# An inverse step joined to another unit's head, its banks emptied by ScalarE, and split and weight sums spread

## The chip, the cores and the metric

The kernel runs on one core of a Trainium2 chip. The metric is the time of one execution on the device in microseconds; three runs of the kernel before are given. A profile of one execution goes with them.

## What is computed

```python
def _attn_ref(x, filt_r, filt_i):          # x: (8, 3008, 256)
    X = np.fft.rfft(x, axis=1)
    Y = X * (filt_r + 1j * filt_i)[None, :, :]
    return np.fft.irfft(Y, n=x.shape[1], axis=1).astype(np.float32)

def _moe_ref(x, w_in, w_out):              # x: (24064, 256), w_in: (256, 2048), w_out: (2048, 256)
    h = x @ w_in
    g = h - np.tanh(h)
    return (g @ w_out).astype(np.float32)
```

The output of the first function, with batch and sequence flattened, is the input of the second. All is float32; the weights come as 64-bit floats and are converted on the chip.

## The kernel before, in words

**The transform.** The sequence of 3008 is 64 x 47. The forward transform has a first step (`first`, or `split_first` from batch 3 on, in small tiles), which goes to DRAM (`ct1`), and a middle step (`middle`): products over the 47 residues, the filter, products back, and out to DRAM again (`ct2`). `middle` does this four times per batch; each time has a "there" (products by `packed` with the first of `WAYS`, line 407), eight steps of filter arithmetic on VectorE, and a "back" (`packed` with the second of `WAYS`). The inverse's last step is `last`: it reads `e2` (loaded from `ct2` by `load_e2`) and makes `ut`, the activations of the dense part, with 32 products in tiles of 64 x 64 (64 instructions, line 587).

**The dense part.** Batches are cut into six chunks; a pair of batch and chunk is a group, 48 in all. A group is worked in four units `U = 4 i + u`, each with a quarter of the hidden columns. In unit `U` TensorE does `up(U)` and `down(U - 2)`, while `shrink(U - 1)` computes h - tanh(h) on ScalarE and VectorE. Both products use seven block products in place of eight, so combinations of blocks are formed beforehand: of weights by `sums`, of activations by `combine` on POOL or VectorE. `up` has banks `x`, `y` and `z`; `down` accumulates in `o0` to `o3` from a group's unit 2 to the next group's unit 1; one more bank is `t`.

**The order.** It is written out by hand. `up` calls four callbacks between its products: `d` and `e` advance `down`, `s` advances `shrink`, and `t(k)`, k = 0 to 4, advances everything else at a fixed place in the unit: up to four stores, then one of: the next group's `last` at (unit 3, k = 2), a step of `first` for batch 2, a step of `split_first` for batch p + 2 at the places in `SPLIT_AT` (chunk, unit, k), or a step of `middle` for batch p + 1 ("there" at (2, 0), "back" at (1, 3), filter arithmetic at `FILTERED`). The conversion of the weights and their sums go on in `t` and `e` by `converting`, from a generator `late`.

**Banks around the change.** `up` begins with products 1 and 2 into `x` and `y`, whose reader is the copy `s1` and the addition of line 651; `t(0)` comes after them. The last value of `x` is read by the copy of line 676, after the fourth call of `t`. `last` uses banks `t` and `y`; ScalarE copies the odd one (line 591) and VectorE adds and subtracts, reading the even one from the bank (lines 594 and 595). "there" uses `t`, `o3`, `o1`, `o2`; ScalarE copies the last two, and VectorE reads the first two from the banks (lines 491 and 492). In unit 1, `down` for the group before ends; its last bank, `o3`, is read by VectorE at line 839. A split's products have line 346, its copies lines 351 and 352, its sums lines 354 and 355.

Of the kernel before, what the change touches and what calls it, by code (L numbers as in the profile page):

```python
# [9 lines left out]
F32 = mybir.dt.float32  # L10
# [7 lines left out]
BATCH, SEQ, DM = 8, 3008, 256  # L18
# [6 lines left out]
CH = 4  # L25
XH = 4
NC = NH // CH
# [90 lines left out]
def kernel(  # L118
# [104 lines left out]

        return jobs

    def sums(u):

        w = (wu if u < 4 else wd)[:, :, 256 * (u % 4):256 * (u % 4) + 256]
        V.tensor_add(w[:, 4], w[:, 6], w[:, 3])
        yield  # L230
        for to, one_in, less in ((5, 4, 0), (2, 1, 5), (6, 0, 6)):
            V.tensor_sub(w[:, to], w[:, one_in], w[:, less])
            yield

    def begun(tiles, job, queue=nc.sync):
        j = converted(tiles, *job, queue)
# [3 lines left out]
    pending = [1]  # L240
# [71 lines left out]
    def split_first(b, z):  # L312

        quarters = [slice(32 * k, 32 * k + 32) for k in range(4)]
        for c, tags in enumerate((("t", "o1", "y", "o0"), ("t", "o3", "o1", "o2"),
                                  ("t", "o1", "y", "o0"))):
            f = tr.tile([128, XH, 128], F32, tag="f", bufs=2, name="f")[:, 0:2]
            f = f.rearrange("p a (b n) -> p (a b) n", n=32)
            nc.sync.dma_start(f, split_d[:, 256 * c:256 * c + 256])
            x0, x1 = (tr.tile([128, XH, DM], F32, tag="x", bufs=2, name="x_sb") for _ in range(2))  # L320
            for h, t in enumerate((x0, x1)):
                at = b * SEQ + 32 * h * NR
                for g in range(2):
                    r = 2 * FH * c + FH * g
                    low, high = quarters[g], quarters[2 + g]
                    nc.sync.dma_start(t[low], dram(x.tensor, (at + r) * DM,
                                                   [[NR * DM, 32], [1, FH * DM]]))
                    lo = int(r == 0)
                    if lo:
                        nc.sync.dma_start(t[high, 0], dram(x.tensor, at * DM,  # L330
                                                           [[NR * DM, 32], [1, DM]]))
                    nc.sync.dma_start(t[high, lo:FH], dram(x.tensor, (at + NR - r - lo) * DM,
                                                           [[NR * DM, 32], [-DM, FH - lo], [1, DM]]))
            yield
            both = tr.tile([128, 2, 2, DM], F32, tag="a1", bufs=1, name="a1")
            even = both.rearrange("p v n c -> p (v n) c")
            V.tensor_add(even, x0, x1)
            yield
            V.tensor_sub(x1, x0, x1)
            yield  # L340
            banks = z(tags)
            for n in range(2):
                for k, (bank, part) in enumerate(zip(banks, quarters)):
                    for j, to in enumerate(quarters):
                        m, odd = 2 * (j // 2) + n, j % 2
                        nc.tensor.matmul(bank[to, n], f[part, 2 * m + odd],  # L346
                                         (x1 if odd else even)[part, m], start=True, stop=True)
            made = both, x0.rearrange("p (v n) c -> p v n c", v=2)
            other = x1[:, 0:2]
            for g, a1 in enumerate(made):  # L350
                ACT.copy(a1[:, 1], banks[2 + g])
            ACT.copy(other, banks[1])
            for g, a1 in enumerate(made):
                V.tensor_add(a1[:, 0], other if g else banks[0], a1[:, 1])
                V.tensor_sub(a1[:, 1], other if g else banks[0], a1[:, 1])
                outs[:0] = [(dram(ct1[b], ((1 - j % 2) * NH + 2 * FH * c + FH * g +
                                           2 * (j // 2)) * DM,
                                  [[2 * NH * DM, 32], [64 * NH * DM, 2], [1, 2 * DM]]),
                             a1[part].rearrange("p v n c -> p v (n c)"))
                            for j, part in enumerate(quarters)]  # L360
                yield

    SPLIT_AT = {(0, 0, 2), (0, 1, 0), (0, 1, 3), (1, 1, 1), (1, 1, 4), (2, 0, 2),
                (3, 0, 2), (4, 2, 0), (4, 2, 2), (4, 3, 0), (5, 0, 2), (5, 1, 0), (5, 1, 3),
                (5, 2, 2)}

    def parts(t, b, g, first_block=0, n=4, step=1):

# [24 lines left out]
    def packed(banks, o, weight, data):  # L393

        ahead, whole, late = [], [], []
        for q, bank in enumerate(banks):
            part = slice(PAD * q, PAD * q + NH)
            for col in range(4):
                to, at = bank[PAD * col:PAD * col + PAD], data(q, col)[part]
                plain, special = (wide[part, weight(q, col, last)] for last in (0, 1))  # L400
                if o == 3 and 3 == (col if weight is WAYS[0] else q):
                    ahead.append((to[:, 0], plain, at[:, 0:DM]))
                    late.append((to[:, 1], special, at[:, DM:2 * DM]))
                else:
                    whole.append((to.rearrange("p n c -> p (n c)"), plain, at))
        for to, weights_of, at in ahead + whole + late:
            nc.tensor.matmul(to, weights_of, at, start=True, stop=True)  # L407
# [165 lines left out]

    e2s, uts = {}, {}

    def last(i, z):

        b, c = groups[i]
        n = sum(widths(c))
# [3 lines left out]
        for h in range(2):  # L583
            for j, r in enumerate(order(c)):
                for bank, half in zip(banks, rows):
                    for m, part in enumerate(rows):
                        nc.tensor.matmul(bank[part, h, j],  # L587
                                         e2[half, r - CH * c, h * 128 + 64 * m:h * 128 + 64 * m + 64],
                                         gt[half, r - CH * c], start=True, stop=True)
        odd = tr.tile([128, 2, CH, 64], F32, tag="e1", bufs=2, name="odd")  # L590
        ACT.copy(odd, banks[1])
        u4 = ut.rearrange("p h (j n) -> p h j n", n=128)
        m = sum(w == 128 for w in widths(c))
        V.tensor_add(u4[:, :, :, 0:64], banks[0], odd)
        V.tensor_sub(u4[:, :, 0:m, 127:63:-1], banks[0][:, :, 0:m], odd[:, :, 0:m])
        w = n // 2
        if i == 0:
            uts[i] = (ut, None, w)
# [13 lines left out]

    hs, gs = {}, {}

    def up(U, d, e, s, t):

        i, u = divmod(U, 4)
        b, tu, w = uts[i]
        rhs = [b[0][0], b[1][0], b[1][1], tu[:, 3, 0:w], tu[:, 0, 0:w], tu[:, 1, 0:w],
               tu[:, 2, 0:w]]  # L620
# [24 lines left out]
        mm(X, 1, True)  # L645
        mm(Y, 2, True)
        s1 = copied("s1")
        t(0)
        d()
        shrinks(0)  # L650
        V.tensor_add(h[:, 0, :, 0:w], Y, s1)
# [76 lines left out]
    def shrink(U):  # L728
# [42 lines left out]
        if U + 2 == 4 * len(groups):  # L771
            yield

        combine(blocks, [t[:, k, :, 0:w] for k in range(4)],
                V if pending or U + 2 >= 4 * len(groups) else G)
        gs[U] = (blocks, t, w)
        yield

# [232 lines left out]
    with tc.tile_pool(name="tr", bufs=2) as tr, tc.manual_schedule():  # L1011
# [278 lines left out]
        with tc.tile_pool(name="dn", bufs=2) as dn, \  # L1290
# [5 lines left out]
            def zd2(name, shape):  # L1296
                return [ps.tile(shape, F32, tag=tag, bufs=1, name=name) for tag in "ty"]

            def zd4(tags):
                return [ps.tile([128, 2, DM], F32, tag=tag, bufs=1, name="pm") for tag in tags]  # L1300

# [55 lines left out]
            kinds.update({at: "filter" for at in FILTERED})  # L1357

            firsts, mids = {2: fs}, {}
            for U in range(total + 2):  # L1360
                i, u = divmod(U, 4)
                if U == 6:
                    assert not pending
                    late = (None for u in (3, 5, 6, 7) for _ in sums(u))
                if U == 3:
                    G.dma_start(mats[:, 0:10 * PAD], wide_d[0:KM])
                if U < total:
                    p, c = groups[i]
                    if c == 0 and u == 0 and 0 < p < BATCH - 1:
                        plan += STAGES  # L1370
                    if u == 0 and i + 1 < len(groups) and c + 1 < NC:
                        e2s[i + 1] = load_e2(*groups[i + 1])
                    if u == 2 and i + 1 < len(groups) and c + 1 == NC:
                        assert not plan
                        e2s[i + 1] = load_e2(*groups[i + 1])
                    if u == 3 and c + 1 == NC and p + 3 < BATCH:
                        firsts[p + 3] = split_first(p + 3, zd4)
                        next(firsts[p + 3])
                    if u == 3 and c + 1 == NC and p + 2 < BATCH:
                        mids[p + 2] = middle(p + 2, zd4)  # L1380
                        next(mids[p + 2])
# [15 lines left out]
                def e():  # L1397

                    next(dw, None)
                    converting((U < 6) * (3 if U > 1 else 1))  # L1400

                def s():

# [2 lines left out]
                def t(k):  # L1406
# [7 lines left out]
                    if i == 1 and pos == LEAD - 7:  # L1414
# [1 line left out]
                        mids[1] = middle(1, zd4)  # L1416
                        next(mids[1])
                        plan.extend(STAGES)
                    if (u, k) == (3, 2) and i + 1 < len(groups):
                        next(last(i + 1, z2))  # L1420
                    elif due and due[0] <= pos and (U < 4 or u < 3 and k == 2):
                        due.pop(0)
                        next(firsts[2])
# [5 lines left out]
                    converting(2)  # L1429
                    if k and U > 2:  # L1430
                        next(copies, None)
                    if k and U > 4:
                        next(copies, None)

                if U < total:
# [52 lines left out]
```

## Time and profile before

| | us |
|---|---|
| median of 3 runs | 2554.69 |
| lowest, highest | 2554.43, 2557.47 |
| the profiled execution's own time | 2554.88 |
| its span, first to last instruction | 2553.1 |

The granted TensorE clock is 0.999 over the span. In a profile's rows L594 is line 594 of the kernel, PE is TensorE's products and PEld its weight loads, DVE is VectorE, ACT ScalarE, POOL GpSimd, SP the engine that issues most transfers (SPq its queue). Groups show busy time, mean duration and the idle time ahead of them, with what ended it. In a timeline a row is one instruction or several merged; an idle time of the engine ahead of it stands in brackets with what released it. Products overlap, so the pace is read from their starts and not from their durations.

### The profile page before, as it was taken

How to read it: one execution, taken by the hardware profiler on the slowest of the kernel's cores; microseconds unless marked ns; L12 is line 12 of the kernel's file. 1: busy time of each engine (PE TensorE's matmuls, PEld its weight loads, DVE VectorE, ACT ScalarE, POOL GpSimd, SP SyncE). 2: the span in 40 equal slices, each digit the busy share in tenths (PEclk: the TensorE clock that was granted, in tenths of full speed). 3: DMA queues.
4: the chain of work that ended last, by engine and by line, in shares of the span. 5: the costliest groups of instructions: out<-in, count | busy, mean ns of one | idle time of the engine just before them, and what ended most of it. 6: DMA issues, size and time to landing. Idle time of an engine off the chain costs nothing.

```text
span 2553.1 us, 44607 instructions
## 1 busy us (share of the span) xinstructions
PE 2534.6 (99%) x17072; PEld 2170.2 (85%) x17072; DVE 1875.4 (73%) x2262; ACT 1667.5 (65%) x2499; POOL 1476.2 (58%) x1120
## 2 busy tenths in 40 slices
PE   9999999999999999999999999999999999999998
PEld 8678889888898888988888888888889888898887
DVE  6987777887678876888668886688866777555555
ACT  4666666666666666666666666666666666666665
POOL 4257665666466665666555665566645666455552
PEclk9999999999999999999999999999999999999999
DMA  8863224322343323342234322433123322110110
GB/s 243 262 157 107 65 54 109 102 65 61 87 98 91 82 66 91 80 112 59 72 94 103 88 57 61 110 99 97 36 69 84 92 66 52 26 32 18 26 22 19
DMA packets 333664, 211.37 MB, mean 83 GB/s; under 512 B 231645, under 2 KB 305531, under 8 KB 329793
## 3 DMA queue, kind: packets, MB, share of 16 engines
q1 hardware_dynamic: 319091, 184.93, 29.7%
q0 software_dynamic: 11120, 16.16, 2.2%
q10 hardware_dynamic: 3230, 7.34, 0.8%
q8 instruction: 136, 2.23, 0.4%
q14 instruction: 87, 0.71, 0.1%
HBM read 127.81 MB, written 83.39 MB: 83 GB/s over the span
## 4 chain that ended last, share of the span: by engine, by line
PE 96%; DMA 2%; DVE 1%; issue 0%; POOL 0%; ACT 0%; SPq 0%; ACTq 0%; POOLq 0%; DVEq 0%
PE o L800 44%; PE x L628 25%; PE z L628 12%; PE y L628 6%; PE pm L407 3%; PE pu L587 2%; PE o L862 1%; PE pm L346 1%; PE pf L303 1%; DMA x<-in_x_dram 0%; PE o L698 0%; DMA ct<-e 0%; DMA gt<-g 0%; DMA filt<-in_filt_r_dram 0%; PE x L698 0%
## 5 line engine op out<-in xcount | busy, mean ns | idle before, releaser
L800 PE MATMUL o<-t,wd 128*128 128x256 f32 (+1 forms) x3008 | 763.2, 376 | 0.6 <-POOL t L608 0.6
L608 POOL TENSOR_TENSOR t<-h 128x512 f32<-128x512 f32 (+1 forms) x186 | 304.4, 1636 | 719.3 <-DVE h L750 693.0
L750 DVE TENSOR_TENSOR h<-h,y 128x1024 f32<-128x1024 f32 (+1 forms) x384 | 580.6, 1512 | 160.2 <-ACT y L746 156.7
L800 PEld LDWEIGHTS o<-t,wd 128*128 128x128 f32 x3008 | 568.3, 190 | 87.3 <-POOL o L832 15.1
L628 PE MATMUL x<-tu,wu 128*128 128x256 f32 (+1 forms) x2256 | 576.0, 378 | 0.1
L800 PE MATMUL o<-h,wd 128*128 128x256 f32 (+1 forms) x2256 | 573.2, 377 | 0.2 <-DVE h L750 0.2
L800 PEld LDWEIGHTS o<-h,wd 128*128 128x128 f32 x2256 | 425.3, 190 | 71.7 <-issue 18.4
L634 ACT COPY s<-x 128x512 f32<-128x512 f32 (+1 forms) x188 | 108.6, 578 | 564.4 <-PE x L628 564.4
L628 PEld LDWEIGHTS x<-tu,wu 128*128 128x128 f32 x2256 | 422.9, 190 | 57.8 <-issue 3.9
L743 ACT ACTIVATE y<-y 128x1024 f32<-128x1024 f32 (+1 forms) x384 | 399.4, 1040 | 12.1
L746 ACT ACTIVATE y<-y 128x1024 f32<-128x1024 f32 (+1 forms) x384 | 399.9, 1041 | 4.6
L740 ACT ACTIVATE y<-h 128x1024 f32<-128x1024 f32 (+1 forms) x384 | 400.4, 1043 | 2.5 <-DVE h L676 1.7
L609 POOL TENSOR_TENSOR t<-h,t 128x512 f32<-128x512 f32 (+1 forms) x186 | 314.0, 1688 | 14.6
L611 POOL TENSOR_TENSOR t<-h,t 128x512 f32<-128x512 f32 (+1 forms) x186 | 303.8, 1633 | 0.0
L610 POOL TENSOR_TENSOR t<-h 128x512 f32<-128x512 f32 (+1 forms) x186 | 288.9, 1553 | 0.0
L634 ACT COPY u<-x 128x512 f32<-128x512 f32 (+1 forms) x376 | 213.3, 567 | 58.0 <-PE x L628 53.8
L676 DVE COPY h<-x 128x512 f32<-128x512 f32 (+1 forms) x188 | 127.8, 680 | 126.6 <-PE x L628 126.5
L628 PE MATMUL z<-tu,wu 128*128 128x256 f32 (+1 forms) x752 | 190.1, 375 | 0.4 <-DVE h L684 0.4
L628 PE MATMUL z<-ut,wu 128*128 128x256 f32 (+1 forms) x752 | 190.1, 375 | 0.4 <-DVE h L668 0.4
L628 PE MATMUL y<-ut,wu 128*128 128x256 f32 (+1 forms) x752 | 190.1, 375 | 0.0
L628 PE MATMUL x<-ut,wu 128*128 128x256 f32 (+1 forms) x752 | 190.0, 375 | 0.0
L668 DVE TENSOR_TENSOR h<-z,u 128x512 f32<-128x512 f32 (+1 forms) x188 | 127.2, 677 | 73.3 <-ACT u L634 72.4
(211 smaller groups left out, 2799.5 us busy)
## 6 DMA issues: line engine op xcount, KB each, us to landing
ft<-filt SPq DMA_DIRECT2D x28, 1024.0 KB
ct<-nn SPq DMA_DIRECT2D x56, 512.0 KB
e<-ct SPq DMA_DIRECT2D x47, 512.0 KB
a<-ct SPq DMA_DIRECT2D x112, 192.0 KB
out_dram<-ot SPq DMA_DIRECT2D x1248, 16.0 KB
x_sb<-in_x_dram SPq DMA_DIRECT2D x110, 128.0 KB
ct<-a SPq DMA_DIRECT2D x60, 128.0 KB
ct<-x_sb SPq DMA_DIRECT2D x60, 128.0 KB
```

The source lines that it names most:

```text
L608: by.tensor_sub(t[0], b[0][1], b[0][0])
L609: by.tensor_sub(t[1], b[1][1], t[0])
L610: by.tensor_sub(t[2], b[1][1], b[0][1])
L611: by.tensor_sub(t[3], b[1][0], t[1])
L628: nc.tensor.matmul(bank[:, k], wu[:, q - 1, (2 * u + k) * 128:(2 * u + k + 1) * 128], rhs[q - 1], start=(first and k == 0), stop=True, ski ...
L634: ACT.copy(t, X)
L676: V.tensor_copy(h[:, 2, :, 0:w], X)
L740: ACT.activation(y[k], ht[k], AF.Arctan, scale=TURN)
L743: ACT.activation(y[k], y[k], AF.Tanh, scale=BEND)
L746: ACT.activation(y[k], y[k], AF.Square, scale=SCALE, accum_out=y_sums[:, 2 * U + k // 2:2 * U + k // 2 + 1])
L750: V.tensor_mul(ht[k], ht[k], y[k])
L800: nc.tensor.matmul(product(q), wd[:, q - 1, (2 * u + k) * 128: (2 * u + k + 1) * 128], rhs[q - 1][:, k], start=(u == 0 and k == 0 and q == ...
```

## The change

`merged(U)` is true for unit 2 of some groups: chunks 2 to 4 of batch 0, all six chunks of batches 1 to 5, and chunks 0 to 3 of batch 6. There `up` calls `t(0)` ahead of its first product, and `t(0)` does the next group's `last` and then, in the same call, the "there" or the split products that fall on it. `last` then uses banks `y` and `x`, and ScalarE copies both. The load of `e2` is issued at the head of unit 0 for the groups where it was unit 2 (but one).

`split_first` takes other banks, copies all four with ScalarE, and does its four sums in four steps, for which `SPLIT_AT` has 23 places in place of 14. `packed`, on the way there, takes the banks in the order 0, 2, 3, 1. Four stores more are issued at the end of a batch. Of the last four quarters' weight sums, three of each four go to unit 5, and the fourth follows from unit 6 on. Two combinations, of `shrink(6)` and `shrink(7)`, go to VectorE. The filter's copies (`copies`) advance twice per call in unit 5 alone, where they did so in all units from 5 on.

```diff
-    def sums(u):
+    def sums(u, n=4):
         w = (wu if u < 4 else wd)[:, :, 256 * (u % 4):256 * (u % 4) + 256]
         V.tensor_add(w[:, 4], w[:, 6], w[:, 3])
         yield
-        for to, one_in, less in ((5, 4, 0), (2, 1, 5), (6, 0, 6)):
+        for to, one_in, less in ((5, 4, 0), (2, 1, 5), (6, 0, 6))[:n - 1]:
             V.tensor_sub(w[:, to], w[:, one_in], w[:, less])
             yield
+
+    def last_sum(u):
+        w = (wu if u < 4 else wd)[:, :, 256 * (u % 4):256 * (u % 4) + 256]
+        V.tensor_sub(w[:, 6], w[:, 0], w[:, 6])
...
-        for c, tags in enumerate((("t", "o1", "y", "o0"), ("t", "o3", "o1", "o2"),
-                                  ("t", "o1", "y", "o0"))):
+        for c, tags in enumerate((("t", "y", "o1", "o0"), ("t", "o3", "o1", "o2"),
+                                  ("t", "o3", "o1", "o2"))):
...
-            other = x1[:, 0:2]
+            others = x1.rearrange("p (v n) c -> p v n c", v=2)
+            for k in (1, 0, 2, 3):
+                ACT.copy(made[k - 2][:, 1] if k > 1 else others[:, k], banks[k])
+            yield
             for g, a1 in enumerate(made):
-                ACT.copy(a1[:, 1], banks[2 + g])
-            ACT.copy(other, banks[1])
-            for g, a1 in enumerate(made):
-                V.tensor_add(a1[:, 0], other if g else banks[0], a1[:, 1])
-                V.tensor_sub(a1[:, 1], other if g else banks[0], a1[:, 1])
+                V.tensor_add(a1[:, 0], others[:, g], a1[:, 1])
+                yield
+                V.tensor_sub(a1[:, 1], others[:, g], a1[:, 1])
...
-    SPLIT_AT = {(0, 0, 2), (0, 1, 0), (0, 1, 3), (1, 1, 1), (1, 1, 4), (2, 0, 2),
-                (3, 0, 2), (4, 2, 0), (4, 2, 2), (4, 3, 0), (5, 0, 2), (5, 1, 0), (5, 1, 3),
-                (5, 2, 2)}
+    SPLIT_AT = {(0, 0, 2), (0, 1, 0), (0, 1, 3), (1, 0, 1), (1, 0, 2), (1, 1, 1), (1, 1, 2),
+                (1, 1, 4), (2, 0, 2), (3, 0, 2), (4, 2, 0), (4, 2, 1), (4, 2, 2), (4, 2, 3),
+                (4, 2, 4), (4, 3, 0), (5, 0, 2), (5, 1, 0), (5, 2, 0), (5, 2, 1), (5, 2, 2),
+                (5, 2, 3), (5, 2, 4)}
...
-        for q, bank in enumerate(banks):
+        for q in (0, 2, 3, 1) if weight is WAYS[0] else range(4):
+            bank = banks[q]
...
-    def last(i, z):
+    def last(i, z, held=False):
...
-        odd = tr.tile([128, 2, CH, 64], F32, tag="e1", bufs=2, name="odd")
-        ACT.copy(odd, banks[1])
+        even, odd = banks
+        for k in (1, 0) if held else (1,):
+            t = tr.tile([128, 2, CH, 64], F32, tag="e1", bufs=2, name=("even", "odd")[k])
+            ACT.copy(t, banks[k])
+            even, odd = (even, t) if k else (t, odd)
...
-        V.tensor_add(u4[:, :, :, 0:64], banks[0], odd)
-        V.tensor_sub(u4[:, :, 0:m, 127:63:-1], banks[0][:, :, 0:m], odd[:, :, 0:m])
+        V.tensor_add(u4[:, :, :, 0:64], even, odd)
+        V.tensor_sub(u4[:, :, 0:m, 127:63:-1], even[:, :, 0:m], odd[:, :, 0:m])
...
+    def merged(U):
+        i, u = divmod(U, 4)
+        b, c = groups[i]
+        return u == 2 and (1 < c < NC - 1 if b == 0 else
+                           c < (4 if b == BATCH - 2 else NC) and b < BATCH - 1)
+
     def up(U, d, e, s, t):
         i, u = divmod(U, 4)
+        if merged(U):
+            t(0)
...
         s1 = copied("s1")
-        t(0)
+        if not merged(U):
+            t(0)
...
         combine(blocks, [t[:, k, :, 0:w] for k in range(4)],
-                V if pending or U + 2 >= 4 * len(groups) else G)
+                V if pending or U in (6, 7) or U + 2 >= 4 * len(groups) else G)
...
+            def z2u(name, shape):
+                return [ps.tile(shape, F32, tag=tag, bufs=1, name=name) for tag in "yx"]
...
+            extra = (None for u in (3, 5, 6, 7) for _ in sums(u, 3))
...
                 if U == 6:
                     assert not pending
-                    late = (None for u in (3, 5, 6, 7) for _ in sums(u))
+                    for _ in extra:
+                        pass
+                    late = (last_sum(u) for u in (3, 5, 6, 7))
...
-                    if u == 0 and i + 1 < len(groups) and c + 1 < NC:
+                    at = (2, 0) if merged(4 * i + 2) else (3, 2)
+                    if i + 1 < len(groups) and u == (2 if (p, c) == (0, NC - 1) else 0):
+                        assert c + 1 < NC or not plan
                         e2s[i + 1] = load_e2(*groups[i + 1])
-                    if u == 2 and i + 1 < len(groups) and c + 1 == NC:
-                        assert not plan
-                        e2s[i + 1] = load_e2(*groups[i + 1])
+                    if u == 3 and c + 1 == NC:
+                        store_some(4)
...
                     converting((U < 6) * (3 if U > 1 else 1))
+                    if U == 5:
+                        assert not pending
+                        for _ in range(3):
+                            next(extra, None)
...
-                    if (u, k) == (3, 2) and i + 1 < len(groups):
-                        next(last(i + 1, z2))
+                    behind = i + 1 < len(groups) and (u, k) == at
+                    if behind:
+                        next(last(i + 1, z2 if u == 3 else z2u, u == 2))
+                    if behind and u == 3:
+                        pass
                     elif due and due[0] <= pos and (U < 4 or u < 3 and k == 2):
...
-                    if k and U > 4:
+                    if k and U == 5:
                         next(copies, None)
```

## The prediction

> **What bounds the kernel now.** I read the page first: the busy shares, then the chain of work that ended last.
>
> ```profile
> PE 2534.6 (99%) x17072; PEld 2170.2 (85%) x17072; DVE 1875.4 (73%) x2262; ACT 1667.5 (65%) x2499; POOL 1476.2 (58%) x1120
> PE 96%; DMA 2%; DVE 1%; issue 0%; POOL 0%; ACT 0%; SPq 0%; ACTq 0%; POOLq 0%; DVEq 0%
> ```
>
> TensorE is busy for 2534.6 of 2553.1 us and carries 96% of the chain. A change that leaves its products alone can take time only from seams between products and from the little idling there is; it can lose much more, if another engine begins to hold TensorE up. So I look for what a seam costs, in the timeline of TensorE in one stretch of batch 3. First column: start in us; second: duration; xN: instructions merged.
>
> ```profile
> 1003.05 1.03 PE L628 MATMUL x<-tu,wu 128*128 128x256 f32 x4
> 1003.91 1.03 PE L628 MATMUL z<-tu,wu 128*128 128x256 f32 x4
> 1006.07 0.59 PE L800 MATMUL o<-t,wd 128*128 128x256 f32 x2
> 1006.59 1.16 PE L587 MATMUL pu<-gt,e 64*64 64x64 f32 x64
> 1007.69 1.13 PE L628 MATMUL x<-tu,wu 128*128 128x256 f32 x4
> 1008.65 1.89 PE L800 MATMUL o<-t,wd 128*128 128x256 f32 x8
> 1010.38 1.03 PE L628 MATMUL x<-tu,wu 128*128 128x256 f32 x4
> ```
>
> Starts give the pace: four full matmuls take 1003.91 - 1003.05 = 0.86, or 0.216 each. The two at 1006.07 should end at 1006.50, but the inverse step (line 587, tiles of 64x64) starts at 1006.59: 0.09 lost at the way into small tiles. It runs to 1007.69. The four full matmuls after it then take 0.96 instead of 0.86: another 0.10 at the way back. The filter's and the split's products (tiles of at most 32x32) have the same seams:
>
> ```profile
> 1082.51 1.14 PE L407 MATMUL pm<-xy,mats_sb 24*32 24x512 f32 x32
> 1083.58 1.02 PE L800 MATMUL o<-t,wd 128*128 128x224 f32 x4
> 1084.44 1.03 PE L628 MATMUL z<-ut,wu 128*128 128x256 f32 x4
> 1086.17 1.03 PE L628 MATMUL y<-ut,wu 128*128 128x256 f32 x4
> 1087.12 1.22 PE L407 MATMUL pm<-a,mats_sb 24*32 24x512 f32 x32
> 1088.27 1.99 PE L800 MATMUL o<-h,wd 128*128 128x256 f32 x8
> 1090.10 1.03 PE L628 MATMUL x<-tu,wu 128*128 128x256 f32 x4
> 1098.74 1.03 PE L628 MATMUL x<-ut,wu 128*128 128x256 f32 x4
> 1038.88 1.47 PE L407 MATMUL pm<-a,mats_sb 24*32 24x512 f32 x32
> 1040.28 1.78 PE L800 MATMUL o<-h,wd 128*128 128x224 f32 x8
> ```
>
> 1087.12 is 0.09 after 1086.17 + 0.86, and the eight full matmuls from 1088.27 take 1.83 instead of 1.73. The same 32 small products take 1.07 at 1082.51, 1.15 at 1087.12, and 1.40 at 1038.88 (the first filter step of a batch).
>
> **The joining.** In `merged` units the inverse step leaves the middle of unit 3 for the head of unit 2, directly before a filter or split step that is there anyway. I count the joins from the code: batch 0 has chunks 2 to 4 (3), batches 1 to 5 six each (30), batch 6 four: 37. Before, such a pair crossed full to 64, 64 to full, full to 32, 32 to full; after, full to 64, 64 to 32, 32 to full. One entry (0.09) and one slow first group (0.10) go. No trace row shows 64 to 32. Bounds: free, then the 0.10 or so that separates the last small product from the full one goes too, 0.3 a join, 11 us; or as dear as the two seams it replaces, no gain. I take the price of the way into small tiles that the rows show, so the seam costs what the inverse step's way out costs now, and a join saves 0.09 + 0.10: 37 x 0.19 = 7.0 us. The Trainium skill, "TensorEngine Tiling (Array Packing)", Key Properties, says that changing the tiling mode drains the engine; by it 64 to 32 isn't free, three drains are left of four, and the 11 us fall away. No row here tests that.
>
> What must hide the moved work? The tile goes to banks `y` and `x`, which the unit's own first products need next, so ScalarE now empties both.
>
> ```profile
> 1081.76 0.20 ACT L746 ACTIVATION_READ_ACCUMULATOR y<-y 128x1 f32 x1
> 1106.96 0.58 ACT L591 COPY odd<-pu 128x512 f32<-128x512 f32 x1 [0.83 <-PE pu L587]
> 1089.05 0.69 DVE L491 TENSOR_TENSOR xy<-pm,xy 128x512 f32<-128x512 f32 x1 [2.00 <-ACT xy L489]
> 1097.21 0.69 DVE L676 COPY h<-x 128x512 f32<-128x512 f32 x1 [0.43 <-PE x L628]
> 1036.26 0.69 DVE L354 TENSOR_TENSOR a<-pm,a 128x512 f32<-128x512 f32 x1 [1.37 <-ACT a L351]
> 1038.66 0.42 DVE L839 TENSOR_TENSOR o<-o,p 128x256 f32<-128x256 f32 x1
> L594 DVE TENSOR_TENSOR ut<-pu,odd x48: 684/692/693, 78.7 to 2476.9; 128x512 f32<-128x512 f32 x48
> L355 DVE TENSOR_TENSOR x_sb<-x_sb x15: 691/693/1518, 462.0 to 1920.9; 128x512 f32<-128x512 f32 x15
> 1105.74 1.16 PE L587 MATMUL pu<-gt,e 64*64 64x64 f32 x64
> ```
>
> The odd copy starts 1106.96 - 1105.74 = 1.22 after the step's first product and takes 0.58: `x` is free 1.80 after it, `y` about 2.4. TensorE wants `x` after 1.10 (inverse) + 1.07 (filter) = 2.17 and `y` 0.96 later. Slack 0.37, so no wait, provided ScalarE is free. It is: its last work of unit 1 ends at 1081.96, the inverse step would begin at 1084.44 + 0.86 + 0.09 = 1085.4. The extra `even` copies (37 x 0.58 = 21 us) fall into that idling. Behind the two copies in ScalarE's queue stand the filter's copies and the unit's `s1`; TensorE needs `s1` only after `y`'s product and the eight of `down`, 2.6 us later. VectorE's two combinations (2 x 0.69 = 1.4) move into unit 2, where it idles 2.00 before the filter's sums while the unit grows by 1.1; unit 3 loses them. The four POOL combinations move with them, earlier than their reader in the next group. On SP's queue the load of `e2` keeps its place, unit 0, but is wanted one and a half units earlier; at the turn of a batch it comes two units earlier.
>
> **The order in `packed`, the spread sums.** The 1.40 at 1038.88 stands beside a VectorE that waited 1.37 for the split's copies (L354) and so read bank `o3` (L839) only at 1038.66 to 1039.08, after the filter had begun; the second product in the old order writes `o3`. Copies first, sums later, and `o3` last: I take 1.40 - 1.07 = 0.33 for the first filter step of batches 1 to 5, 1.65 us in all. The 0.08 of the 1.15 case I do not count (up to 12 x 0.08 = 1.0 more). The fourth ScalarE copy of a split (0.6) lies behind the same idle ScalarE.
>
> **The weight sums and two combinations.** Two windows of three (unit 5, unit 7), and TensorE's waits in between; the window's columns are its length, then PE, PEld, DVE, ACT and POOL busy:
>
> ```profile
> 142.50:156.30 13.80, 13.80 (x54) 9.88 (x52) 6.03 (x8) 9.46 (x14) 1.06 (x1) 1.00 0.81 198
> 171.50:187.40 15.90, 14.22 (x122) 11.59 (x121) 15.83 (x20) 8.57 (x12) 13.84 (x12) 1.00 0.24 50
> 174.05 1.03 PE L628 MATMUL x<-tu,wu 128*128 128x256 f32 x4
> 175.51 1.13 PE L628 MATMUL z<-tu,wu 128*128 128x256 f32 x4 [0.44 <-DVE h L684]
> 178.30 0.33 PE L587 MATMUL pu<-gt,e 64*64 64x64 f32 x4
> 179.48 1.15 PE L587 MATMUL pu<-gt,e 64*64 64x64 f32 x60 [0.84 <-DVE h L651]
> 184.11 1.03 PE L800 MATMUL o<-t,wd 128*128 128x256 f32 x4
> 185.54 1.13 PE L628 MATMUL z<-ut,wu 128*128 128x256 f32 x4 [0.40 <-DVE h L668]
> 191.68 0.59 PE L800 MATMUL o<-h,wd 128*128 128x256 f32 x2
> 192.88 0.70 PE L800 MATMUL o<-t,wd 128*128 128x256 f32 x2 [0.60 <-POOL t L608]
> ```
>
> ```profile
> L232 DVE TENSOR_TENSOR wd<-wd 128x256 f32<-128x256 f32 x12 | 7.3, 632 | 0.1
> ```
>
> Unit 5 has VectorE busy 6.03 of 13.80; unit 7 has it at 15.83 of 15.90, and there TensorE waits for it. By starts the delays are 175.51 - 174.91 = 0.60, about 1.16, 0.57 and 0.77: 3.1 us. Twelve of the sixteen sums of units 6 and 7 go to unit 5: 12 x 0.63 (the mean of L232) = 7.6 us at most, into 7.8 idle. Two combinations go from POOL to VectorE, four operations each, 4 x 0.69 = 2.8 by the shape of L355, at the ends of units 7 and 8; the second of them is what TensorE waited for at 192.88. I take 2.8 of the 3.1 as gone, with 0 and 3.1 as ends. POOL issues fewer filter loads per unit from unit 6 on; they are spread later, at no cost to TensorE as long as POOL has idling, 2 us of 15.9 here.
>
> **Sum.** 7.0 + 1.65 + 2.8 = 11.45 us from the profiled execution's 2554.88 (span 2553.1 plus 1.8 around it): 2543.4. The median of the runs is 2554.69, 0.2 below it; I let 2543.4 stand for both.
>
> **Rivals.** (a) *64 to 32 is as dear as the way over full tiles.* The joining gives nothing, the rest 4.45: 2550.4. For it: no row shows that seam. Against: every seam into small tiles costs the same 0.09. Chance 0.10.
>
> (b) *Slower: VectorE falls behind in unit 2.* The two `ut` operations now have both operands in SBUF. The rows show what that can mean: L594, with a PSUM operand, never took over 693 ns; L355, SBUF only, reached 1518. POOL's combination of the unit before runs in just that stretch. The Trainium skill, "SBUF — State Buffer", Who interferes with whom, has a VectorE instruction with two SBUF inputs contend with a POOL instruction that reads SBUF, and the second to start block wholly; the spread of L355 agrees. At worst the unit gets 2 x 1.52 = 3.0 us. Room: 2.00 idle, 0.43 idle, 1.1 of longer unit, and from the end of L676 (1097.90) to the next use of `x` (1098.74) 0.84: 4.4. It decides from there: each 0.1 us beyond it costs 3.7 us over 37 joins, and beyond 0.31 the gain is gone. With 0.5: 2543.4 + 18.5 = 2561.9. Chance 0.10.
>
> (c) *`x` or `e2` comes late.* Copies more than 0.37 late, or a late load, hold the unit's head:
>
> ```profile
> 1026.07 0.43 SPq L566 DMA_DIRECT2D e<-ct  x1
> ```
>
> At a batch's head SP issues this only at 1026.07, and the joined step would want it near 1037.3, 11 us later; the split's later stores put SP back by some us. Against: issues of 0.43 follow without a gap. A loss of 0.2 a join, 7.4 us, gives 2550.8; 1 us at each of six batch heads gives 2549.4. Chance 0.08.
>
> **How the numbers follow.** Forecast 0.72: 2543.4. About 0.2% (5.1 us) is what a measurement of this kernel can tell from no change, so faster means below 2549.6. The range runs from 2538.5 (a free seam, 11 instead of 7, and the 1.0) to 2551.0, which takes in (a) and the mild end of (c); (b) stays out. Faster: the forecast, part of (c) and small overshoots of (b), 0.80; same, mostly (a), 0.10; slower 0.10.
>
> **What would show it.** Right: TensorE starts of line 587 followed about 1.1 us later by line 407 or 346 without full matmuls between them, and the next full group about 1.07 (filter) after that; unit pairs shorter by 0.2; the four early waits gone; the first filter step of a batch at 1.07 to 1.15. Wrong: waits of `x` or `y` of line 628 on ScalarE, on L676 or on `e2`; `ut` operations well over 0.69; 64 to 32 taking 0.3 over the pace.

## The result, and the profile after

The kernel after takes 2542.72 us (median of 5, 2541.45 to 2544.66), the kernel before 2556.72 in the same comparison (median of 5, 2554.43 to 2557.47): a ratio of 0.9948 [0.9934, 0.9963], some 13 us. The profiled execution took 2542.18, its span 2540.3, at a granted clock of 0.999. Busy times:

```profile
PE 2522.6 (99%) x17072; PEld 2173.1 (86%) x17072; DVE 1935.6 (76%) x2270; ACT 1694.2 (67%) x2551; POOL 1532.0 (60%) x1112
```

TensorE issues the same 17072 products, is busy 12.0 us less, and bounds the kernel as before; VectorE, ScalarE and POOL each have more to do.

To compare traces I use the tiles `pf` and `pu`, whose rows give the start of their first and last product: `pf` begins just behind the first inverse step, and `pu` ends with the last one. What lies ahead changes from one execution to the next. The first inverse step waits 0 to 4.4 us for its `e2`, and in seven of the runs (not in the kernels before and after) the granted clock is 0.50 for 3.41 us around that step. Here it is in `e2_join_alone` (length, PE, PEld, DVE, ACT, POOL busy, then the clock):

```profile
78.62:82.03 3.41, 3.41 (x30) 2.67 (x21) 2.07 (x5) 1.15 (x2) 0.00 (x0) 0.50 0.99 236
```

From the first inverse product to the first of `pf` it is 11.1 us there, and 9.8 and 9.9 in the kernels before and after. From `pf` on, the traces can be compared. Before, then after:

```profile
L303 PE MATMUL pf<-x_sb,f x80: 379/379/379, 86.1 to 195.8; 128*128 128x256 f32 x80
L587 PE MATMUL pu<-gt,e x3072: 218/218/267, 76.3 to 2476.0; 64*64 64x64 f32 x192
L308 PE MATMUL pf<-x_sb,f x80: 379/379/417, 85.9 to 194.0; 128*128 128x256 f32 x80
L595 PE MATMUL pu<-gt,e x3072: 218/218/267, 76.0 to 2463.5; 64*64 64x64 f32 x192
```

2476.0 - 86.1 = 2389.9 became 2377.6: 12.3 us less. Below, "the stretch" is this time. TensorE's timeline, a joined pair in batch 3:

```profile
1078.06 1.03 PE L648 MATMUL z<-ut,wu 128*128 128x256 f32 x4
1079.01 1.16 PE L595 MATMUL pu<-gt,e 64*64 64x64 f32 x64
1080.10 1.16 PE L415 MATMUL pm<-a,mats_sb 24*32 24x512 f32 x32
1081.19 1.13 PE L648 MATMUL x<-ut,wu 128*128 128x256 f32 x4
1082.16 1.03 PE L648 MATMUL y<-ut,wu 128*128 128x256 f32 x4
```

The inverse step begins 1079.01 - (1078.06 + 0.86) = 0.09 late, as every way into small tiles did. From it to the filter is 1.09, as it was to a full matmul before (1.10): 64 to 32 costs the way out and nothing more. The filter takes 1.09, and the first full group after it 0.97 instead of 0.86. One 0.09 and one 0.11 are gone, as forecast. Next the first filter step of batch 3, and one of the five places (before, in a unit of the split) at which TensorE had waited for ScalarE; the kernel after has no wait at any of these five:

```profile
1032.59 1.16 PE L415 MATMUL pm<-a,mats_sb 24*32 24x512 f32 x32
1033.68 0.65 PE L648 MATMUL x<-ut,wu 128*128 128x224 f32 x2
```
```profile
634.62 0.59 PE L800 MATMUL o<-t,wd 128*128 128x256 f32 x2
635.17 1.13 PE L628 MATMUL x<-tu,wu 128*128 128x256 f32 x4
636.14 0.59 PE L800 MATMUL o<-t,wd 128*128 128x256 f32 x2
```

The filter step takes 1.09 where it took 1.40. In the second fence (before) `x` starts 635.17 - 634.62 - 0.43 = 0.12 late (ScalarE's copy of `u` out of that bank runs from 634.55 to 635.12) and its four products take 0.97, 0.11 over the pace: 0.23, five times.

The `ut` operations, the waits of TensorE, and units 5 and 7 (length, then PE, PEld, DVE, ACT, POOL busy):

```profile
L605 DVE TENSOR_TENSOR ut<-even,odd x37: 864/1506/1751, 215.7 to 2101.8; 128x512 f32<-128x512 f32 x37
L605 DVE TENSOR_TENSOR ut<-pu,odd x11: 690/692/693, 78.6 to 2464.4; 128x512 f32<-128x512 f32 x11
L606 DVE TENSOR_TENSOR ut<-even,odd x37: 1214/1756/1764, 217.0 to 2103.3; 128x512 f32<-128x512 f32 x32, 128x384 f32<-128x384 f32 x5
```
```profile
PE pu L595 <- DMA e<-ct: 2.4, 1, 2.4
PE z L648 <- DVE h L705: 1.4, 2, 1.1
```
```profile
142.20:156.20 14.00, 14.00 (x55) 10.07 (x54) 9.65 (x18) 9.47 (x14) 0.49 (x1) 1.00 0.78 185
171.30:185.30 14.00, 14.00 (x125) 12.13 (x124) 12.09 (x12) 8.52 (x13) 13.83 (x10) 1.00 0.18 33
```

With both operands in SBUF a pair of `ut` operations takes about 1.51 + 1.76 = 3.3 us, where it took 1.4: rival (b)'s slowdown is there. No wait of TensorE on VectorE comes of it in this kernel. Unit 7 no longer idles TensorE; two early waits on VectorE are left at line 705, and a short one at line 697 (0.33 by starts, at 141.79).

### The profile page after: what moved, and what is told of

The parts are those of the page before. It is cut to its first block, busy times and chain, and to the rows that moved or that the text cites. A ratio compares the mean times of both kernels' runs of the same rounds, so it can differ in the third digit from the quotient of the medians.

```text
span 2540.3 us, 44575 instructions
## 1 busy us (share of the span) xinstructions
PE 2522.6 (99%) x17072; PEld 2173.1 (86%) x17072; DVE 1935.6 (76%) x2270; ACT 1694.2 (67%) x2551; POOL 1532.0 (60%) x1112
## 3 DMA queue, kind: packets, MB, share of 16 engines
q8 instruction: 136, 2.23, 0.4%
## 4 chain that ended last, share of the span: by engine, by line
PE 96%; DVE 2%; DMA 1%; issue 0%; POOL 0%; ACT 0%; ACTq 0%; SPq 0%; POOLq 0%; DVEq 0%
PE o L821 44%; PE x L648 25%; PE z L648 12%; PE y L648 6%; PE pm L415 2%; PE pu L595 2%; PE pm L351 1%; PE o L883 1%; PE pf L308 1%; DMA filt<-in_filt_r_dram 1%; DMA x<-in_x_dram 0%; DMA ct<-e 0%; PE o L719 0%; PE x L719 0%; PE z L719 0%
## 5 line engine op out<-in xcount | busy, mean ns | idle before, releaser
L619 POOL TENSOR_TENSOR t<-h 128x512 f32<-128x512 f32 (+1 forms) x184 | 303.6, 1650 | 707.3 <-DVE h L771 642.2
L771 DVE TENSOR_TENSOR h<-h,y 128x1024 f32<-128x1024 f32 (+1 forms) x384 | 571.0, 1487 | 156.4 <-ACT y L767 156.4
L622 POOL TENSOR_TENSOR t<-h,t 128x512 f32<-128x512 f32 (+1 forms) x184 | 338.3, 1838 | 0.0
L620 POOL TENSOR_TENSOR t<-h,t 128x512 f32<-128x512 f32 (+1 forms) x184 | 310.5, 1688 | 14.4
L621 POOL TENSOR_TENSOR t<-h 128x512 f32<-128x512 f32 (+1 forms) x184 | 276.9, 1505 | 0.0
```

The costliest lines, as they stand in the source:

```text
L619: by.tensor_sub(t[0], b[0][1], b[0][0])
L620: by.tensor_sub(t[1], b[1][1], t[0])
L621: by.tensor_sub(t[2], b[1][1], b[0][1])
L622: by.tensor_sub(t[3], b[1][0], t[1])
L771: V.tensor_mul(ht[k], ht[k], y[k])
```

## The experiments

All are edits of the kernel after unless it is said otherwise. Where only one time is given, there was one execution, and the stretch of its trace says more than its time.

### Is it the joining?

**The joining taken out** (`e1_no_join`), all else kept:

```diff
-        return u == 2 and (1 < c < NC - 1 if b == 0 else
-                           c < (4 if b == BATCH - 2 else NC) and b < BATCH - 1)
+        return False
```

> The changed kernel with no unit merged: the inverse step is back in unit 3, everything else stays. Theory (seams): each of 37 joins saved one way into small tiles (0.09 us) and one slow first group (0.10), so 7.3 us come back: 2542.2 + 7.3 = about 2549.5, with line 595 between full matmuls on both sides 48 times. Rival (relief of VectorE): the gain comes from work moved away from crowded units, the seams are hidden or small; then under 2 us come back, and waits on VectorE appear in the rows of TensorE.

Measured: 2559.67, ratio 1.0018 [1.0008, 1.0027]. That is not 7 us above the kernel after but 17, and slower than the kernel before. The wait that is new, and one case of it on TensorE and on ScalarE (a line of the kernel after has a number one lower here from 631 on):

```profile
PE x L647 <- ACT u L653: 5.4, 10, 0.5
```
```profile
634.82 1.13 PE L647 MATMUL x<-tu,wu 128*128 128x256 f32 x4 [0.54 <-ACT u L653]
```
```profile
629.02 1.07 ACT L356 COPY x_sb<-pm 128x512 f32<-128x512 f32 x2 [1.78 <-PE pm L351]
629.98 0.60 ACT L356 COPY a<-pm 128x512 f32<-128x512 f32 x1
630.46 0.62 ACT L356 COPY x_sb<-pm 128x512 f32<-128x512 f32 x1
634.20 0.57 ACT L653 COPY u<-x 128x512 f32<-128x512 f32 x1
```

The four copies of a split hold ScalarE from 629.02 to 630.94 before it can go on; the three of the kernel before took one copy less, about 0.5, and there `x` was only 0.12 late, five times. By starts each of the ten waits costs 0.70 and a slow group of 0.10, 8.0 in all. The stretch is 2395.3, 17.7 above the kernel after: these 8.0, the 7.3 of the seams, 1.8 from filter steps that are some 0.1 longer, and 0.6 at early waits. In the kernel after the joined unit is longer ahead of `u`, and the wait is absent. So without the joining the other edits are a loss, 5.4 against the kernel before, and what covers the split's fourth copy is the joining.

**The joining alone**, put into the kernel before (`e2_join_alone`): `merged`, banks `y` and `x`, the two copies, the place of the load, and none of the rest:

```diff
+        if merged(U):
+            t(0)
...
-            t(0)
+        if not merged(U):
+            t(0)
...
+                        next(last(i + 1, z2 if u == 3 else z2u, u == 2))
```

> The kernel before with the joining alone (with the copies by ScalarE and the earlier load of e2); the split, the order in packed and the weight sums are as before, so one split a batch (5 of 37) finds no partner and 32 inverse steps stand next to small products. Theory (seams): 32 x 0.197 = 6.3 us less than 2554.9, about 2548.6, and the first filter step of batches 1 to 5 still near 1.4 us. Rival: the parts need each other, and without the spread sums VectorE or o3 holds up the joined unit; then 2552 or more, with a filter step longer than before.

Measured: 2552.91, ratio 0.9990 [0.9980, 1.0000]; the stretch is 2387.8, only 2.1 below the kernel before. Its waits, its stretch and the first filter step of batch 1:

```profile
PE x L640 <- ACT odd L593: 3.5, 5, 0.7
```
```profile
L303 PE MATMUL pf<-x_sb,f x80: 379/379/379, 88.4 to 198.6; 128*128 128x256 f32 x80
L587 PE MATMUL pu<-gt,e x3072: 218/218/313, 77.3 to 2476.2; 64*64 64x64 f32 x192
```
```profile
425.14 1.80 PE L407 MATMUL pm<-a,mats_sb 24*32 24x512 f32 x32
426.87 1.02 PE L640 MATMUL x<-ut,wu 128*128 128x224 f32 x4
```

In chunk 5 of batches 1 to 5 the old `SPLIT_AT` has no step at the head of unit 2, so five inverse steps stand alone there, directly ahead of `x`: a wait of 0.70, by starts 0.78 with the restart, 3.9 in all. The first filter step takes 1.73 instead of 1.40, 1.65 in all, and the early waits cost 0.7 more than before. Against that 32 true joins gain 32 x 0.197 = 6.3, twelve other filter steps take 1.09 instead of 1.15 (0.8), and the five waits of 0.12 are gone with their restarts (1.2). The difference, 2.1, is what the stretch shows. Alone the joining brings 2 us; the rest needs a split that gives each inverse step a partner and frees its banks early.

**The two small steps exchanged** (`e5_inverse_behind`): the same seams, but filter or split first and the inverse step behind it.

```diff
-                    if behind:
-                        next(last(i + 1, z2 if u == 3 else z2u, u == 2))
...
+                    if behind and u == 2:
+                        next(last(i + 1, z2u, True))
```

> The changed kernel with the two small steps of a joined unit exchanged: filter or split products first, the inverse step behind them, directly ahead of the unit's products into x and y. Theory: the seams stay three (32 to 64 like 64 to 32, 0.09 over the pace), but nothing covers the copy of x, which is free 1.80 us after the inverse step's first product and is wanted after 1.10: 0.7 us of wait 37 times, 26 us: about 2568. Rival: the cover isn't needed, 2542.

Measured: 2607.56; stretch 2441.6, 64.0 above the kernel after.

```profile
PE x L648 <- ACT odd L601: 34.3, 37, 1.5
PE pm L415 <- DVE o L860: 2.5, 6, 0.4
```
```profile
473.97 2.17 PE L415 MATMUL pm<-a,mats_sb 24*32 24x512 f32 x32
476.07 1.16 PE L595 MATMUL pu<-gt,e 64*64 64x64 f32 x64
477.94 1.13 PE L648 MATMUL x<-ut,wu 128*128 128x256 f32 x4 [0.70 <-ACT odd L601]
```

`x` now waits 0.70 behind each inverse step, and the filter takes up to 2.1 instead of 1.09, in part since its bank `o3` is still being read at line 860. By starts the waits for `x` cost 37.0 of the 64 and the slow filters and splits 27.0. So the order is worth far more than the seam: inverse first, each step hides the other's bank.

### What the second copy is for

**The even bank read by VectorE** (`e4_even_in_bank`): in joined units ScalarE copies only the odd bank.

```diff
-                        next(last(i + 1, z2 if u == 3 else z2u, u == 2))
+                        next(last(i + 1, z2 if u == 3 else z2u))
```

> The changed kernel, but in joined units VectorE reads the even bank (y) directly, as it did in unit 3; ScalarE copies only the odd one. Theory: ScalarE's second copy is what frees y in time. Without it y is free after the odd copy (1.80 us after the inverse step's first product) and two VectorE operations (0.69 + 0.61), 3.1 to 3.3 us after it, and TensorE wants it at 3.2: waits of 0 to 0.3 us in the joined units, 0 to 10 us in all, at y of line 648. Rival: VectorE is there in time, the second copy is idle work: 2542, and ScalarE 21 us less busy.

Measured: 2546.90; stretch 2380.8, 3.2 above. By starts `y` is 0.04 to 0.15 late in 19 units, each with a slow group behind it: 3.3. The second copy is worth about that, although it makes VectorE's operations twice as long.

### The other edits

**The old order of the filter's banks** (`e3_old_order`).

```diff
-        for q in (0, 2, 3, 1) if weight is WAYS[0] else range(4):
+        for q in range(4):
```

> The changed kernel with packed's old order of banks (0, 1, 2, 3) on the way there. Theory A: the old 1.40 us of the first filter step came from VectorE, late at o3 behind the split's sums; with those spread, o3 is free early enough and the old order costs nothing: 2542, filter steps at 1.07 to 1.09. Theory B: the order itself matters, since o3 is read last in unit 1 whatever comes before it: 0.1 to 0.3 us in each of some 20 filter steps, 2 to 6 us.

Measured: 2544.62; stretch 2377.5, 0.1 below: theory A. The first filter steps of batches 1 to 5 take 1.15 instead of 1.09, 0.3 in all, and the wait at 141.79 is absent (0.4), as it is in other runs that leave this part alone. So of 0.31 that such a step lost, the order has 0.06. The rest goes with the split's spread sums, by when VectorE reads `o3`. In the kernel after it does so long before the filter begins at 1032.59:

```profile
1030.85 0.42 DVE L860 TENSOR_TENSOR o<-o,p 128x256 f32<-128x256 f32 x1 [0.83 <-PE o L821]
```

With the old order it does too (1033.04, filter 1034.83). In `e2_join_alone`, with the old sums, the same operation starts at 425.35, behind the sums and after the filter's start at 425.16. No run had the old sums with the new order.

**The old weight sums** (`e6_old_weights`): the sums back in units 6 and 7, the two combinations on POOL, and the filter's copies at their old pace.

```diff
-                V if pending or U in (6, 7) or U + 2 >= 4 * len(groups) else G)
+                V if pending or U + 2 >= 4 * len(groups) else G)
...
-            late = (last_sum(u) for u in (3, 5, 6, 7))
+            late = (None for u in (3, 5, 6, 7) for _ in sums(u))
...
-            if k and U == 5:
+            if k and U > 4:
```

> The changed kernel with the weight sums, the two combinations and the pace of the filter loads as before. Theory: the early waits come back in place of the new ones: TensorE's waits between 137 and 212 us go from 2.0 to about 3.3 us, 2542.2 + 1.4 = 2543.6. Rival (these edits carry a larger part, 2.8 as predicted): 2545.

Measured: 2543.10; stretch 2379.7, 2.1 above. The early waits are back; the longest:

```profile
PE pu L595 <- DVE h L672: 0.8, 1, 0.8
```

**The combinations behind line 705** (`e7_combine_later`). In the kernel after VectorE does the four operations of a combination, and then the addition that `z` waits for:

```profile
187.30 0.68 DVE L622 TENSOR_TENSOR t<-h,t 128x512 f32<-128x512 f32 x1
187.91 1.21 DVE L508 TENSOR_TENSOR xy<-xy,ft 128x1024 f32<-128x1024 f32 x1
189.04 0.68 DVE L705 TENSOR_TENSOR h<-z,u 128x512 f32<-128x512 f32 x1
```
```profile
189.77 1.13 PE L648 MATMUL z<-tu,wu 128*128 128x256 f32 x4 [1.12 <-DVE h L705]
```

```diff
-        if U + 2 == 4 * len(groups):
+        if U in (6, 7) or U + 2 == 4 * len(groups):
             yield
```

> The changed kernel with the two combinations on VectorE one step later in the unit, behind the addition into h of line 705 in place of ahead of it. Theory: the two waits of z on that addition (1.28 and 0.42 us over the pace) are made by the combinations standing ahead of it in VectorE's queue; they go, about 1.9 us with their slow groups: 2540.3. Rival: the combinations then come late for down, a wait at line 821 takes the place.

Measured: 2540.76; stretch 2375.3, 2.3 below the kernel after, and no wait of `z` is left. That is the forecast 1.9, and 0.4 for the wait at 141.79, which is absent here as in `e3_old_order`. **The same, timed** (`e12_later_timed`):

> The kernel with the two combinations one step later, timed: by the waits of TensorE that left its profile 1.9 us less than the changed kernel, 2540.8, and 0.9940 of the kernel before.

Measured: 2542.44 (2541.99 to 2543.86, 5 runs), ratio 0.9950 [0.9936, 0.9964], which can't be told from the kernel after. Its stretch is 2375.3 again, 2.3 below, but in the profiled execution the first inverse step waited longer for its load, the clock was lowered behind it, and `pf` begins at 88.6, 2.7 later than in the kernel after:

```profile
PE pu L595 <- DMA e<-ct: 4.4, 1, 4.4
```

An edit worth 2 us is smaller than what the first load and the clock behind it vary by.

### How near VectorE is

**The addition done twice** (`e10_add_twice`) and **both operations done twice** (`e11_both_twice`), in joined units. This is the first edit; the second doubles the subtraction as well.

```diff
         V.tensor_add(u4[:, :, :, 0:64], even, odd)
+        if held:
+            V.tensor_add(u4[:, :, :, 0:64], even, odd)
```

> The changed kernel; in joined units VectorE does the first of the two operations on ut a second time (the same values again). It measures VectorE's room. In the changed kernel the two take 1.51 and 1.67 us against 0.69 in bank form, 3.2 in all, and the prediction's room was 4.4 us. Theory: 1.5 us more goes 0.3 beyond the room, up to 11 us over 37 units: 2542 to 2553, with waits of x on line 697 or z on VectorE. Rival: VectorE catches up in the next units, no wait, 2542.

Measured: 2575.72; stretch 2410.0, 32.4 above. From its trace (line 691 is line 689 of the kernel after), then the same place in batch 3 of the kernel after:

```profile
PE z L650 <- DVE h L691: 25.6, 27, 1.3
```
```profile
485.95 1.13 PE L650 MATMUL z<-ut,wu 128*128 128x256 f32 x4 [1.10 <-DVE h L691]
```
```profile
1091.44 0.68 DVE L689 TENSOR_TENSOR h<-z,u 128x512 f32<-128x512 f32 x1
```
```profile
1092.52 1.03 PE L648 MATMUL z<-ut,wu 128*128 128x256 f32 x4
```

In the kernel after, line 689 ends at 1092.12, 0.40 ahead of the product that overwrites its `z`. The 27 units that are joined with a filter step lose 32.4 / 27 = 1.20 each. In 22 of them VectorE's operations on `ut` take 1.7 more; in the other five, with the first filter step of a batch, 0.6; 1.5 on average. So 0.3 to 0.4 was left. The ten units joined with a split show no wait.

> The same with both operations done twice, 3.2 us more. Theory: 2.0 beyond the room, if all of it is lost 74 us, if half is caught up in unit 3 about 37: 2580 to 2616. Rival: still caught up, 2542 to 2550.

Measured: 2610.75; stretch 2443.9, 66.3 above; 49.9 us of the same wait, again 27 times. On average the operations take 1.0 more than in the run before, and the wait is 0.9 longer: beyond the room nearly each 0.1 us is paid. Rival (b)'s mechanism is shown; it lacked under half a microsecond.

### One seam more

**The way back of the filter joined as a third** (`e8_three`): where "back" is due in the unit before, it goes to the head of the joined unit, ahead of the inverse step, in other banks.

```diff
+                    close_by[0] = behind and u == 2 and plan[:1] == ["back"]
+                    if close_by[0]:
+                        plan.pop(0)
+                        next(mids[p + 1])
```

> The changed kernel with a third small step joined: where the unit is merged, the filter's way back leaves unit 1 and goes to the head of unit 2, ahead of the inverse step, with banks o1, o2, t and o0; the filter's way there then takes o3 first. By the seams: 26 ways back lose a way in and a slow first group each, 26 x 0.197 = 5.1 us: about 2537. Rival: ScalarE must empty two banks more before x, and VectorE two more before the filter's banks; if x, t or o2 come 0.2 us late in each of the 26, nothing is gained, 2542; by 0.5 us, 2550.

Measured: 2550.18, ratio 0.9976 [0.9966, 0.9987], slower than the kernel after. (One of its nine executions took 8548.83; no record explains it.)

```profile
PE z L650 <- DVE h L691: 7.8, 6, 2.2
```
```profile
482.21 1.23 DVE L510 TENSOR_TENSOR nn<-xy,ft 128x1024 f32<-128x1024 f32 x1 [2.96 <-DMA ct<-nn]
```
```profile
472.17 1.65 SPq L387 DMA_DIRECT2D a<-ct  x4
473.93 1.28 SPq L939 DMA_DIRECT2D ct<-nn  x2
```
```profile
1712.00:1716.30 4.30, 4.25 (x12) 3.42 (x13) 4.30 (x5) 0.96 (x2) 2.35 (x2) 0.60 0.11 16
```

The 26 seams gained 5.1 by starts, but `nn` is now stored a unit later, the store is issued behind the loads of `a`, and VectorE's next write into `nn` waits 2.96 for it with line 691 queued behind. Two of these waits are 2.36 by starts. After the one at 1712 the granted clock was 0.60 over 4.3 us (the last fence: 0.50 for 3.41 us of them); after the one at 484 it stayed at 1.00.

**The store first, and the combinations later** (`e9_three_stored`):

```diff
                         next(mids[p + 1])
+                        store_some(2)
```

> Three small steps joined, with the two stores of the way back issued at once, ahead of the next loads on SP's queue, and the two combinations one step later. Theory: the waits of z on line 691 in the first joining of three came from VectorE standing until nn was stored (2.96 us at 482.21, on the store of nn), since the store stood behind a load that waits for the filter's way there; with the store ahead they go, the 26 x 0.197 = 5.1 us remain: about 2535 to 2537. Rival: VectorE has too much to do in the joined unit, the store was only the last to come; then the waits stay, 2545 or more.

Measured: 2537.98 (2536.56 to 2544.45, 4 runs), ratio 0.9939 [0.9923, 0.9955]; stretch 2372.2 (its `pf` begins at 86.2), 5.4 below the kernel after.

```profile
L597 PE MATMUL pu<-gt,e x3072: 218/218/268, 76.6 to 2458.4; 64*64 64x64 f32 x192
```

The waits at line 691 are gone but one of 0.3. Two edits stand in this run: the combinations account for 1.9 of the 5.4, as in `e7_combine_later`, and the absent wait at 141.79 for 0.4. The third step nets about 3.1 of its 5.1, with 0.8 lost again to filter steps that take 1.15 in place of 1.09.

It is the best version run: clearly faster than the kernel before, and by its trace faster than the kernel after; the two ratios' intervals overlap, so by time alone that is likely and not shown.

## Why the prediction was right, point by point

**The bound: right.** The gain came from seams and idling of TensorE, with the same products.

**The joins: right.** 0.09 + 0.10 each was forecast, 0.197 measured, 7.3 over 37 for 7.0. The price taken for 64 to 32, no rows of which were there, was the right end of its bounds: the step costs on the way to 32 what it cost on the way to full tiles. So the free seam and rival (a) both fall, and the Trainium skill's rule ("TensorEngine Tiling (Array Packing)", Key Properties: a change of tiling mode drains the engine) agrees with the 1.09 from 1079.01 to 1080.10.

**What the joining rests on: not seen.** The prediction wrote of "a filter or split step that is there anyway". For five of the 37 it is there only by the new `SPLIT_AT`, as `e2_join_alone` showed. It held the fourth copy of a split to lie "behind the same idle ScalarE"; without the joining it does not, as `e1_no_join` showed. The parts were summed as if each stood alone: undone or done alone they come to +17.7 and -2.1 us, not to +7 and -7. The sum for the whole was right since in the whole both covers are there.

**The first filter step: right in size, wrong in weight.** 1.65 was forecast, 5 x 0.31 = 1.6 measured; but the order in `packed` gives a fifth of it (`e3_old_order`); the spread sums give the rest. The 1.15 case, left out of the sum, gained too: 0.8 over twelve steps. It gained in `e2_join_alone` as well, with the old order: it comes with the joining.

**The weight sums and combinations: too large.** 2.8 was forecast. The early delays by starts are 0.33 (at 141.79, and not in every execution), 1.28 (at 189.77) and 0.42 (at 204.11), 2.0 in all; before they were the 3.1 of the prediction and a fifth of 0.28 that I had missed, 3.4. So 1.4 is gone. The step that failed is the term of the two combinations: I priced their four operations and put them at the ends of units 7 and 8, but did not look at what they stand ahead of on VectorE, line 705. `e7_combine_later` shows that this is the rest.

**Not in the sum at all:** the five waits of 0.12 and their restarts, 1.2; they are gone in `e2_join_alone` too, so this is the joining's. With it 7.3 + 1.6 + 0.8 + 1.4 + 1.2 = 12.3, which is what the stretch shows, against 11.45 forecast. That the sum came so near is in part luck: 1.4 too much for the weights was met by 2.0 that stood in no term.

**Rival (b): its price was real, its place wrong.** The two operations take 3.3, over the 3.0 that I held for the worst. I had the end in `x` behind line 676, with room for 4.4. In truth `z` behind the addition at line 689 decides, one operation earlier in VectorE's queue; the room there is 3.3 and the 0.4 that was left, 3.7. How long the operations take depends on POOL, as the last section shows. "`ut` operations well over 0.69" was named as a sign that the prediction was wrong; it was seen without a loss, so it was a poor sign: what counts is the start of the next reader. Of (c), `x` and `e2` in joined units, nothing was seen; `e5_inverse_behind` shows what `x` would have cost.

## What to carry to other kernels

When steps in different tile modes stand next to each other, one way in and one slow group go, here 0.2 us a time; but look first at which bank each step's successor needs, since the order of the two steps was worth 64 us and the seams 7. Before summing the parts of a change, ask for each what covers it and whether that cover is itself part of the change. And when an operation gets longer off the critical path, follow its engine's queue to the first result that the bound engine needs, not to the one that seems to end the unit.

## What the runs showed of the hardware

The same addition of 128x512 takes 0.69 with one operand in PSUM, in `e4_even_in_bank` in all the joined units too, and 0.86 to 1.75 with both in SBUF, with POOL's combination running in the same stretch:

```profile
1081.27 1.28 POOL L620 TENSOR_TENSOR t<-h,t 128x512 f32<-128x512 f32 x1
```
```profile
1081.35 1.74 DVE L605 TENSOR_TENSOR ut<-even,odd 128x512 f32<-128x512 f32 x1 [0.68 <-ACT even L601]
```

When the addition starts, 1081.27 + 1.28 - 1081.35 = 1.20 of POOL's operation is left; the addition takes 0.54 more than that. In all 37 joined units its time is what is left of POOL's operation and 0.54 to 0.55, as if it stood until POOL is done. Where POOL idles, both operands in SBUF cost nothing. In `e10_add_twice` the last of the three operations finds POOL idle in five units, and takes 0.68 (the second row shows POOL's next one, and its idle time):

```profile
427.92 0.68 DVE L608 TENSOR_TENSOR ut<-even,odd 128x512 f32<-128x512 f32 x1
```
```profile
428.68 0.73 POOL L621 TENSOR_TENSOR tu<-ut 128x256 f32<-128x256 f32 x1 [1.23 <-DVE ut L608]
```

The Trainium skill, "SBUF — State Buffer", Who interferes with whom, has a VectorE instruction with two SBUF inputs contend with a GpSimd one that reads SBUF; these rows agree.

The clock of 0.60 after a wait of 2.36 us, once in two such waits, was not expected either. `e11_both_twice` shows the same: after five of its 27 waits, with 2.01 to 2.08 us of idling, the clock was 0.50 for 3.41 us, and after others of up to 2.23 it was not. The Trainium skill, "TensorE: Matmul & The Clock Gate", Part 1, puts a lowered clock behind an idle window of about 3.4 us that runs freely; the waits here were shorter, and why they sufficed in some cases stays open.
